# Two small reads of the first DFT pieces ahead of ScalarE's first instruction, in an FNet plus Mixer kernel

## Chip, cores and metric

The kernel runs on one core of one Trainium2 chip. The metric is device microseconds of one launch. The change is judged by the median of several runs of each kernel. 0.3% of the time before is 2.6 us.

## What is computed

One input x of 2048 tokens by 640 channels is normalized along its channels. The output is x plus a Fourier mixing of the normalized rows plus a token-mixing MLP of the same rows, all in 32-bit floats. Cut to what matters:

```python
xn = layernorm(x)                        # 2048 x 640
a  = xn @ dft_hid_re.T ; b = xn @ dft_hid_im.T
fnet = dft_seq_re @ a - dft_seq_im @ b   # dft_seq: 2048 x 2048 each
u  = gelu(xn.T @ w1 + b1)                # w1: 2048 x 1728
mlp = (u @ w2 + b2).T                    # w2: 1728 x 2048
out = x + fnet + mlp
```

## The kernel before

TensorE does nearly all the arithmetic. The kernel runs the Fourier mixing over the sequence first, then over the channels, then the two layers of the MLP ("up", "down"). Every weight piece is split into a rounded part ("hi", written by ScalarE, line 143) and a remainder ("lo", written by VectorE, line 146), and a product is three matmuls: hi by hi, hi by lo, lo by hi.

The DFT matrix of the sequence lies in device memory as `dft_seq[8][16][128][512]`. The first index is the column block of the real part (0 to 3) or the imaginary part (4 to 7), the second is a block of 128 rows. One piece is `dft_seq[c, i]`, 128 x 512 floats, 256 KB, contiguous; `dft_seq[0, 0]` and `dft_seq[1, 0]` are 4 MB apart. The change reads from these two. They are also the first two pieces that the kernel loads: `load(0)` (line 484) brings `dft_seq[0, 0]`, and the load of line 586 named `B11`, q = 0, brings `dft_seq[1, 0]`.

The order of the start is written out by hand in `START` (line 42), and the scheduler keeps it (`tc.manual_schedule()`). Each word is one step, and a step puts instructions on several engines. The words that matter here:

- `x0`: two transfers on SyncE's queue (SP), the left and right half of the first 128 rows of x (line 520). `b0`: the load of `dft_seq[0, 0]`. `W1-1-0`: the load of `dft_seq[1, 0]`. Then x1, b1, x2, W1-1-1, b2, W1-1-2, x3, b3 and so on, all on SP in this order.
- `M0 A0`: the moments of the first rows (VectorE, lines 218 and 221). `R0`: their inverse root (ScalarE, line 227). `G0 O0 V0`: small factors on GpSimd (lines 241, 238, 246, 247).
- `D0`: VectorE normalizes the first 256 columns of the first rows (line 383, `first_hi`). `H0`: ScalarE normalizes 128 more (line 275), with the offset that GpSimd computes in line 238.
- `T0`: hi of the first piece, half of it by ScalarE (line 143), half by VectorE (line 193). `B0`: its lo (VectorE, line 146). `T1`, `B1`: the same for the second piece, hi wholly by ScalarE.
- `P0-0-1`: the first six real matmuls (line 496), hi and lo of the piece against hi of the rows. `P1-0-1`: six for the second piece (line 656). `M1 A1`: the moments of the next rows. `L0`: lo of the first rows (VectorE, line 146, written to tile `n`). `P0-2`, `P1-2`: the passes that need L0.

Before these steps the kernel sets a few constants, lets ScalarE load its table with one tiny activation (line 135), and lets TensorE run 11 matmuls of a constant (line 140, `WARM`), which need no data and whose result is not used.

Of the kernel before, what the change touches and what calls it, by code (L numbers as in the profile page):

```python
# [8 lines left out]
F32 = mybir.dt.float32  # L9
# [5 lines left out]
P = 128  # L15
# [55 lines left out]
def fnet_plus_mixer(  # L71
# [30 lines left out]
    nc = tc.nc  # L102

    keep = ctx.enter_context(tc.tile_pool(name="keep", bufs=1))
# [25 lines left out]
    y_part = [[dram.tile([P, ND, CH], F32, name=f"y{m}{c}") for c in range(NC)] for m in range(2)]  # L130


    nc.vector.memset(one, 1.0)
    nc.gpsimd.memset(eps, EPS)
    nc.scalar.activation(one, one, AF.Abs_reciprocal_sqrt)
# [1165 lines left out]
```

## Time and profile before

| | us |
|---|---|
| median of 3 runs (lowest, highest) | 864.72 (864.64, 866.59) |
| the profiled execution's own time | 864.75 |
| its span, first to last instruction | 862.9 |
| outside the span | 1.85 |
| TensorE busy in the span | 858.4 |
| VectorE, ScalarE, GpSimd busy | 696.6, 529.1, 179.7 |

Times in the views are counted from the start of the span. PE is TensorE's matmul, PEld its weight load, DVE is VectorE, ACT ScalarE, POOL GpSimd. SPq and ACTq are the instruction queues of SyncE and ScalarE where they issue transfers. In a timeline, a row gives start, duration, engine, line, operation, tile written and tile read with their shapes, the number of instructions merged, and in brackets how long the engine had been idle before the row and what ended that idle time. The names in_x and in_dft_seq are the inputs in device memory, pieces the tile into which pieces of the DFT matrix are loaded, piece the tile with its hi and lo.

### The profile page before, as it was taken

The page shows a single profiled execution, that of the slowest core. Times are in us where ns is not written, and L with a number is a line of the kernel's source. Part 1 is how long each engine was busy: PE and PEld are TensorE (multiplying, and loading weights), DVE is VectorE, ACT ScalarE, POOL GpSimd, SP SyncE. Part 2 cuts the span into 40 slices and gives each one's busy share as a digit, 9 for nine tenths or more (in the row PEclk, how much of TensorE's full clock was granted, in tenths as well). Part 3 has the DMA queues.
Part 4 walks back from the last instruction along what each step waited for, and adds up shares of the span by engine and source line. Part 5 has one row for each costly group of instructions (what it writes and reads, how often), then busy time and mean ns, then how long its engine had stood idle before and what let it go on. Part 6 is the DMA issues. An engine that isn't in the chain of part 4 may idle for free.

```text
span 862.9 us, 13981 instructions
## 1 busy us (share of the span) xinstructions
PE 858.4 (99%) x4883; PEld 786.5 (91%) x4883; DVE 696.6 (81%) x1172; ACT 529.1 (61%) x987; POOL 179.7 (21%) x249
## 2 busy tenths in 40 slices
PE   9999999999999999999999999999999999999998
PEld 6888888888888888889999999999999999999998
DVE  7998868784757888877887788888678978897887
ACT  7766676755445555657565556676577856555654
POOL 5333222212121211122100101111312321101211
PEclk9999999999999999999999999999999999999999
DMA  8889594989593746779576766664688779766786
GB/s 316 287 223 322 126 298 130 246 196 297 139 262 61 200 97 144 171 128 211 122 170 169 159 147 181 196 180 152 148 178 186 169 213 243 184 139 130 157 167 149
DMA packets 93350, 159.44 MB, mean 185 GB/s; under 512 B 9408, under 2 KB 37824, under 8 KB 92928
## 3 DMA queue, kind: packets, MB, share of 16 engines
q0 software_dynamic: 26432, 60.40, 38.4%
q1 hardware_dynamic: 66704, 98.06, 35.3%
q8 instruction: 38, 0.62, 0.3%
q14 instruction: 32, 0.26, 0.1%
q10 hardware_dynamic: 144, 0.08, 0.0%
HBM read 102.05 MB, written 61.70 MB: 190 GB/s over the span
## 4 chain that ended last, share of the span: by engine, by line
PE 99%; DMA 0%; SPq 0%; ACT 0%; DVE 0%; issue 0%; DVEq 0%
PE psum L656 44%; PE psum L155 18%; PE psum L154 18%; PE psum L157 17%; PE psum L496 2%; DMA pieces<-in_dft_seq 0%; SPq L520 0%; ACT piece L143 0%; DVE pair L957 0%; DVEq L1297 0%
## 5 line engine op out<-in xcount | busy, mean ns | idle before, releaser
L146 DVE TENSOR_TENSOR piece<-pieces,piece 128x512 fp32r<-128x512 f32 (+4 forms) x514 | 338.7, 660 | 138.6 <-ACT piece L143 135.3
L143 ACT ACTIVATE piece<-pieces 128x512 fp32r<-128x512 f32 (+3 forms) x490 | 306.5, 626 | 230.8 <-PE psum L656 98.1
L656 PE MATMUL psum<-piece,n 128*128 128x512 f32 x1656 | 376.9, 389 | 0.0
L656 PEld LDWEIGHTS psum<-piece,n 128*128 128x128 f32 x1656 | 310.6, 188 | 65.1 <-DVE piece L146 0.4
L155 PE MATMUL psum<-sup,piece 128*128 128x320 f32 x392 | 120.8, 309 | 0.0
L154 PE MATMUL psum<-sup,piece 128*128 128x320 f32 x392 | 120.8, 309 | 0.0
L155 PE MATMUL psum<-sdown,piece 128*128 128x320 f32 x392 | 120.8, 309 | 0.0
L154 PE MATMUL psum<-sdown,piece 128*128 128x320 f32 x392 | 120.8, 309 | 0.0
L149 DVE TENSOR_TENSOR pieces<-pieces 128x512 f32<-128x512 f32 (+3 forms) x146 | 116.5, 803 | 2.8
L469 POOL DMA_DIRECT2D y<-c x76 | 65.5, 898 | 251.4 <-DVE c L692 132.4
L157 PE MATMUL psum<-sup,piece 128*128 128x320 f32 x368 | 113.7, 309 | 0.0
L157 PE MATMUL psum<-sdown,piece 128*128 128x320 f32 x368 | 113.7, 309 | 0.0
L157 PE MATMUL psum<-shid,piece 128*128 128x320 f32 x280 | 86.5, 309 | 0.0
L155 PE MATMUL psum<-shid,piece 128*128 128x320 f32 x280 | 86.5, 309 | 0.0
L154 PE MATMUL psum<-shid,piece 128*128 128x320 f32 x280 | 86.5, 309 | 0.0
L154 PEld LDWEIGHTS psum<-sup,piece 128*128 128x128 f32 x392 | 73.6, 188 | 0.0
L155 PEld LDWEIGHTS psum<-sdown,piece 128*128 128x128 f32 x392 | 73.6, 188 | 0.0
L155 PEld LDWEIGHTS psum<-sup,piece 128*128 128x128 f32 x392 | 73.6, 188 | 0.0
L154 PEld LDWEIGHTS psum<-sdown,piece 128*128 128x128 f32 x392 | 73.6, 188 | 0.0
L1038 POOL DMA_DIRECT2D out<-pair x38 | 33.0, 942 | 189.0 <-DVE pair L952 157.3
L965 ACT ACTIVATE pair<-psum 128x320 f32<-128x320 f32 x101 | 44.0, 436 | 42.4 <-PE psum L157 39.3
L157 PEld LDWEIGHTS psum<-sup,piece 128*128 128x128 f32 x368 | 69.1, 188 | 0.0
(120 smaller groups left out, 863.7 us busy)
## 6 DMA issues: line engine op xcount, KB each, us to landing
pieces<-in_dft_seq SPq DMA_DIRECT2D x136, 256.0 KB, 5.5
y<-c POOLq DMA_DIRECT2D x106, 256.0 KB, 6.1
pieces<-in_w SPq DMA_DIRECT2D x88, 256.0 KB, 4.0
out<-pair POOLq DMA_DIRECT2D x38, 320.0 KB, 5.3
pieces<-y SPq DMA_DIRECT2D x32, 320.0 KB, 4.2
pieces<-in_w SPq DMA_DIRECT2D x32, 192.0 KB, 3.0
up<-pair POOLq DMA_DIRECT2D x8, 640.0 KB, 3.4
pair<-in_x SPq DMA_DIRECT2D x12, 320.0 KB, 4.7
```

Source lines behind the costliest of these rows:

```text
L143: nc.scalar.activation(hi, src, AF.Copy)
L146: nc.vector.tensor_sub(lo, src, hi.bitcast(F32))
L149: nc.vector.tensor_sub(to, a, b)
L154: nc.tensor.matmul(psum, wh, mh, start=first, stop=False, skip_group_check=True)
L155: nc.tensor.matmul(psum, wh, ml, start=False, stop=last and wl is None, skip_group_check=True)
L157: nc.tensor.matmul(psum, wl, mh, start=False, stop=last, skip_group_check=True)
L469: nc.gpsimd.dma_start(y_part[m][c][:, j, :], t, accum_op=ALU.add)
L496: nc.tensor.matmul(to, (hi, hi, lo)[k], w[k % 2], start=k == 0 and i == 0, stop=k == 2 and i % 4 == 3, skip_group_check=True,)
L656: nc.tensor.matmul(to, (hi, hi, lo)[k], w[k % 2], start=k == 0 and begin, stop=k == 2 and q == 3, skip_group_check=True,)
L965: nc.scalar.activation(c, b, AF.Copy)
L1038: nc.gpsimd.dma_start(out_rows[ts[i]], c[:, i, :], accum_op=ALU.add)
```

## The change

Three lines are added ahead of the first instruction of the program's body. A small tile `touched` is taken in on-chip memory (16 partitions, two times 16 floats). ScalarE issues two transfers into it: 64 bytes out of every eighth row of `dft_seq[0, 0]`, 16 rows in all, and the same of `dft_seq[1, 0]`. No instruction reads the tile. They stand ahead of ScalarE's tiny activation and its table load. Nothing else is changed.

```diff
     y_part = [[dram.tile([P, ND, CH], F32, name=f"y{m}{c}") for c in range(NC)] for m in range(2)]
 
 
+    touched = keep.tile([P // 8, 2, 16], F32, name="touched")
+    for c in range(2):
+        nc.scalar.dma_start(touched[:, c, :], dft_seq[c, 0, ::8, :16])
     nc.vector.memset(one, 1.0)
     nc.gpsimd.memset(eps, EPS)
     nc.scalar.activation(one, one, AF.Abs_reciprocal_sqrt)
```

## Rows read from the trace of the kernel before

**Rows 1.** The page, chain that ended last, shares of the span by engine.
```profile
PE 99%; DMA 0%; SPq 0%; ACT 0%; DVE 0%; issue 0%; DVEq 0%
```

**Rows 2.** That chain in order of time: start us, us, what.
```profile
1.66 3.87 DMA pieces<-in_dft_seq
...
7.70 1.38 PE psum L656 x6
9.08 0.86 PE psum L496 x3
```

**Rows 3.** Busy time by stretch: length, then PE, PEld, DVE, ACT, POOL, PEclk, DMA share, GB/s.
```profile
10.60:859.50 848.90, 848.90 (x4855) 781.59 (x4853) 690.13 (x1156) 523.13 (x976) 175.48 (x234) 1.00 0.74 184
```

**Rows 4.** Timeline of PE, start of the span.
```profile
0.79 4.85 PE L140 MATMUL psum<-const-bfloat16-1.0 128*128 128x512 bf16 x11 [0.79 <-PEq L1290]
...
6.02 1.69 PE L496 MATMUL psum<-piece,n 128*128 128x512 f32 x6 [0.37 <-ACT piece L143]
```

**Rows 5.** Busy time by half microsecond, columns as in rows 3; read the last two.
```profile
2.00:2.50 0.50, 0.50 (x3) 0.20 (x2) 0.00 (x0) 0.24 (x2) 0.00 (x0) 1.00 0.71 259
...
3.00:3.50 0.50, 0.50 (x3) 0.17 (x2) 0.47 (x1) 0.00 (x0) 0.00 (x0) 1.00 1.14 159
3.50:4.00 0.50, 0.50 (x3) 0.15 (x1) 0.50 (x2) 0.00 (x0) 0.00 (x0) 1.00 0.88 270
4.00:4.50 0.50, 0.50 (x2) 0.15 (x1) 0.22 (x2) 0.15 (x1) 0.16 (x1) 1.00 1.02 197
4.50:5.00 0.50, 0.50 (x2) 0.15 (x1) 0.32 (x1) 0.15 (x1) 0.28 (x2) 1.00 0.99 346
...
10.00:20.00 10.00, 10.00 (x45) 8.21 (x44) 9.74 (x26) 8.57 (x18) 7.84 (x18) 1.00 1.05 393
```

**Rows 6.** Timeline of SP's queue, start of the span.
```profile
0.75 0.86 SPq L520 DMA_DIRECT2D x<-in_x  x2
...
3.55 0.43 SPq L522 DMA_DIRECT2D x<-in_x  x1
...
5.54 0.40 SPq L522 DMA_DIRECT2D x<-in_x  x1
6.17 0.42 SPq L484 DMA_DIRECT2D pieces<-in_dft_seq  x1
```

**Rows 7.** Timeline of ACT, start of the span.
```profile
0.75 1.28 ACT L135 ACT_TABLE_LOAD   x1 [0.75 <-PEq L1290]
2.05 0.20 ACT L135 ACTIVATE one<-one 128x1 f32<-128x1 f32 x1
4.35 0.29 ACT L227 ACTIVATE near<-mv,eps 128x1 f32<-128x1 f32 x1 [2.10 <-DVE mv L221]
...
5.87 0.48 ACT L275 ACTIVATE n<-x,near 128x128 fp32r<-128x128 f32 x1
6.25 0.62 ACT L143 ACTIVATE piece<-pieces 128x512 fp32r<-128x512 f32 x1
```

**Rows 8.** Timeline of DVE, start of the span.
```profile
3.04 0.97 DVE L218 BATCH_NORM_STATS2 st<-x 128x6 f32<-128x320 f32 x2 [2.15 <-DMA x<-in_x]
...
4.68 0.41 DVE L383 TENSOR_SCALAR n<-x,mv,near 128x256 fp32r<-128x256 f32 x1 [0.43 <-ACT near L227]
5.55 0.29 DVE L193 CAST piece<-pieces 128x256 fp32r<-128x256 f32 x1 [0.46 <-DMA pieces<-in_dft_seq]
...
7.51 0.88 DVE L218 BATCH_NORM_STATS2 st<-x 128x6 f32<-128x320 f32 x2
...
8.55 0.57 DVE L146 TENSOR_TENSOR n<-x,n 128x256 fp32r<-128x256 f32 x2
```

**Rows 9.** Timeline of POOL, start of the span.
```profile
4.75 0.39 POOL L238 TENSOR_SCALAR near<-mv,near 128x1 f32<-128x1 f32 x1 [0.22 <-ACT near L227]
```

**Rows 10.** Timeline of ACT's queue, end of the span.
```profile
860.23 0.37 ACTq L1128 DMA_DIRECT2D out<-pair  x1
```

**Rows 11.** Busy time by stretch at the end, columns as in rows 3; read PE and PEclk.
```profile
859.40:860.00 0.60, 0.21 (x2) 0.00 (x0) 0.35 (x2) 0.00 (x0) 0.00 (x0) 1.00 0.67 237
...
862.00:862.90 0.90, 0.00 (x0) 0.00 (x0) 0.00 (x0) 0.00 (x0) 0.00 (x0) 0.65 0.00 0
```

## The prediction

> **What bounds the kernel now.** I read the chain that ended last first, because it says which engine an edit must reach to matter. 99% of it is PE [rows 1]. The busy time by stretch then says from where on: from 10.60 to 859.50 us PE is busy for all of 848.90 us [rows 3]. Whatever the change does can therefore count only ahead of 10.6 us, by moving PE's real work earlier or later as a whole. At most what PE loses there can be won.
>
> PE runs its 11 matmuls of a constant from 0.79 to 5.64 us, stands idle for 0.37 us, and begins the real work at 6.02 us, when ScalarE has made the hi of the first piece [rows 4]. Six matmuls of 512 columns take 1.38 us in the next group [rows 2]. The first six took 1.69 us [rows 4], so 0.31 us is lost in them, waiting for the lo of the piece. The three of P0-2 take 0.86 us from 9.08 us [rows 2], where half of 1.38 is 0.69: 0.17 us lost, waiting for L0, whose two instructions start at 8.55 us on VectorE [rows 8]. Together PE loses 0.37 + 0.31 + 0.17 = 0.85 us after its constant matmuls. That is the ceiling of a gain that leaves the constant matmuls alone: 0.1% of the time.
>
> Behind the first wait is the load of `dft_seq[0, 0]`: issued at 1.66 us, landed 3.87 us later, at 5.53 us [rows 2]. The second piece is nearly as late. SP's issue of b3 at 6.17 us and that of x3 at 5.54 us [rows 6] come just when the transfers eight places before them have landed: x3 is SP's eleventh, b0 its third. So W1-1-0, the fourth, landed at about 6.16 us, and ScalarE takes it at 6.25 us [rows 7].
>
> The reason for the slow landing is seen in the DMA columns of the half microseconds [rows 5]. From 10 to 20 us the engines are busy (share 1.05) and move 393 GB/s. From 3.0 to 4.5 us they are as busy (1.14, 0.88, 1.02) but move 159, 270 and 197 GB/s. The missing parts, (1 - 159/393) x 0.5 + (1 - 270/393) x 0.5 + (1 - 197/393) x 0.5, are 0.30 + 0.16 + 0.25 = 0.71 us of the engines' time. In 4.5 to 5.0 us, at 346 GB/s, only 0.06 us is missing. The dip of 3.0 to 4.0 (0.46 us) falls where the first piece follows x0's 320 KB, that of 4.0 to 4.5 (0.25 us) where the second piece follows. I read the dips as a price of the first access to each of the two places, 4 MB apart. The rows fit this; they don't prove it.
>
> **The change, part by part.**
>
> ScalarE's two issues. ACT's own row for a transfer has 0.37 us [rows 10], SP's first two took 0.86 us together [rows 6]. So 0.74 to 0.86 us are put ahead of the table load, which took 1.28 us from 0.75 us, and the activation of 0.20 us behind it [rows 7]. They end at 3.0 to 3.1 us instead of 2.25. The next work of ScalarE starts at 4.35 us [rows 7]. The cover is ScalarE's idle time of 2.10 us ahead of it, of which some 1.3 us remain. The cost is nothing; without the cover it would be 0.86 us on the way to the inverse root.
>
> SP's places. If ACT's transfers share SP's turn of eight, x2 (SP's seventh) waits for the first read, W1-1-1 for the second. x2 is issued at 3.55 us [rows 6]. The reads are issued at about 0.75 and 1.2 us. By x0's first half, which was issued at 0.75 and there at 3.04 us (2.3 us) [rows 6, 8], they land at 3.1 and 3.5 us: no wait. By the first piece (3.87 us) they land at 4.6 and 5.1 us, and SP would stand for some 1.1 us with W1-1-1, b2 and all later loads behind it. The engines then still have the pieces and x1 in hand, as the second piece alone lands at 6.16 us, so this too costs next to nothing.
>
> What the reads do to the transfers. The first is issued 0.9 us ahead of the first piece (0.75 against 1.66 us). If the dips are first accesses, the pieces go at the full rate and land up to 0.71 us earlier. But the price does not vanish, it moves to 1.8 us, where x0 is on the same engines. Call d the time by which x0 comes later. Lower end: 0, if the stalls run beside x0's own start. Upper end: 0.71 us, if every stall stands in x0's way in full. The nearest row is x0's start itself, also a first access: 259 GB/s in 2.0 to 2.5 us [rows 5], a loss of (1 - 259/393) x 0.5 = 0.17 us. I take d = 0.2 us, since the reads start in the same microsecond as x0's and wait beside them.
>
> What is late next. With early pieces, VectorE's D0 ends at 4.68 + 0.41 = 5.09, its half of the hi at 5.09 + 0.29 = 5.38 us [rows 8]; later by d, that is 5.6 us, still inside the constant matmuls, so PE's 0.37 us go. But PE soon meets L0, at the end of the order H0 (ACT), T1 (ACT), B1, M1, A1, L0 (DVE). H0 starts at 5.87 us behind T0, T1 at 6.25 us [rows 7]. H0 needs the offset from GpSimd, ready at 4.75 + 0.39 = 5.14 us [rows 9], so it can move up by 0.73 - d. T1 needs the second piece, which comes up by 0.71 - d. M1 starts at 7.51 us right behind its neighbours [rows 8], and x1 moves up with the others. So L0, and PE with it, gains the smaller: 0.71 - d = 0.5 us. After that no wait on PE is known until the end [rows 3].
>
> The sum: 864.75 (the profiled execution: span 862.9 and 1.85 around it) - 0.5 = 864.2 us. Its own time is 0.03 us from the median, so the forecast for a median is the same, 864.2 us. The tile itself takes 128 bytes of a partition and has no reader; the last wait of the kernel comes 850 us after its transfers.
>
> **The rivals.**
>
> The stall is only moved, in full. If the reads hold up the engines as long as the pieces did, d = 0.71 us and the gain is 0. The second piece's stall (0.25 us) then also stands ahead of the first piece, which lay behind it before: b0 lands 0.25 us later. Time: 864.75 to 865.0 us. For it: the engines' share is near 1 while the rate is low [rows 5], so a stalled engine seems to do nothing else. Against it: x0's start costs only 0.17 us. The Trainium skill, "DMA: Bandwidth & Descriptors", section "Issuing engines are not separate DMA queues", speaks for this rival: transfers from ScalarE and SyncE end up on the same 16 engines and interleave, so issuing from a second one saves issue time alone. By that rule the time is this rival's, 864.75 to 865.0 us.
>
> The change doesn't do what it says. If the dips come from the load of the moment, or the reads warm nothing for the other queue, b0 and W1-1-0 are as slow as before and only d remains: 0 to 0.2 us, so 864.75 to 864.95 us. For it: nothing in the trace names the cause of the dips. Against it: from 10 to 20 us the same kind of loads run at 393 GB/s without a dip [rows 5]. The Trainium skill, "HBM Reference", section "Latency", gives 0.2 us for an access on average and 2 us under high load, which would make it load; the rows differ, as the slow stretch is the one that moves less.
>
> The clock falls, the one that ends clearly slower. The 11 constant matmuls take 4.85 us, 0.44 us each, the later ones of the same width 0.23 us [rows 4, 2]: the 1.2 and the 2.4 GHz level. At the end of the kernel PE is done at 859.6 us and the granted clock, a mean of 0.65 from 862.0 to 862.9, has fallen only then [rows 11], after at least 2.4 us of rest. If x0 or b0 came so late that PE rested for 2.4 us rather than 0.37, it would lose 2.0 us by the wait and, if the lower level lasted 4.85 us again, half of that: 864.75 + 2.0 + 2.4 = 869.2 us. It decides from 2.0 us of delay on, nearly three times the whole of the dips.
>
> **How the numbers follow.** Forecast (a gain of 0.25 to 0.85 us, d up to 0.45): 0.55. Stall moved in full: 0.20. No effect: 0.20. Clock: 0.02. What I haven't thought of: 0.03, of which 0.02 slower. The range reaches from the ceiling (864.75 - 0.85 = 863.9) to the full stall (865.0). The three runs before spread from 864.64 to 866.59, so a median of few runs may stray by some tenths: 863.6 to 865.4 us. About 0.3%, 2.6 us, is what a measurement of this kernel can tell from no change, so all but the last cases count as the same: faster 0.01, same 0.95, slower 0.04.
>
> **What would show it.** Right: the first piece lands by 4.9 us, the rate from 3.0 to 4.5 us is near 390 GB/s, a dip stands at 1.8 to 2.5 us instead, PE's idle time of 0.37 us is gone and L0 starts near 8.05 us. Full stall: x0's first statistics start 0.5 us or more after 3.04 us, and b0 lands no earlier. No effect: the same dips at 3.0 to 4.5 us. ScalarE's cover is wrong if the inverse root starts late while the moments were ready. The prediction is wrong altogether if PE waits after 10.6 us or its clock falls.

## The result, and the profile after

The change made the kernel slower: a median of 867.52 us (867.09 to 868.06, 9 runs) against 865.12 us (864.44 to 866.59, 9 runs) of the kernel before in the same rounds, a ratio of 1.0029 with an interval of 1.0020 to 1.0038. That is 2.4 us more, where 0.5 us less was forecast, and outside the range of 863.6 to 865.4 us. The profiled execution took 867.61 us with a span of 865.7 us, 2.8 us more than the span before.

The start looks as the forecast wanted it. All lines of the changed kernel behind the added ones count three higher; in the experiments it is as many as each adds. First PE's timeline, which answers to [rows 4], then ACT's [rows 7], then DVE's [rows 8], all of the changed kernel:

```profile
0.79 4.75 PE L143 MATMUL psum<-const-bfloat16-1.0 128*128 128x512 bf16 x11 [0.79 <-PEq L1293]
5.51 1.68 PE L499 MATMUL psum<-piece,n 128*128 128x512 f32 x6
```

```profile
0.75 0.89 ACTq L135 DMA_DIRECT2D touched<-in_dft_seq  x2
1.67 1.28 ACT L138 ACT_TABLE_LOAD   x1 [1.67 <-PEq L1293]
...
4.42 0.29 ACT L230 ACTIVATE near<-mv,eps 128x1 f32<-128x1 f32 x1 [1.26 <-DVE mv L224]
4.69 0.42 ACT L146 ACTIVATE piece<-pieces 128x256 fp32r<-128x256 f32 x1
5.25 0.49 ACT L278 ACTIVATE n<-x,near 128x128 fp32r<-128x128 f32 x1
5.65 0.62 ACT L146 ACTIVATE piece<-pieces 128x512 fp32r<-128x512 f32 x1
```

```profile
3.02 1.06 DVE L221 BATCH_NORM_STATS2 st<-x 128x6 f32<-128x320 f32 x2 [2.14 <-DMA x<-in_x]
...
8.11 0.63 DVE L149 TENSOR_TENSOR n<-x,n 128x256 fp32r<-128x256 f32 x2
```

The first piece is there when ScalarE asks for it at 4.69 us, PE begins its real work at 5.51 instead of 6.02 us, and L0 comes at 8.11 instead of 8.55 us. So some 3.2 us must have been lost later. No view of waits shows it. After the start of the program PE waits for nobody; this is the whole list of its waits in the changed kernel (what it waited for, us in total, times, longest):

```profile
PE psum L143 <- PEq L1293: 0.8, 1, 0.8
```

The loss is in the number of matmuls that a busy stretch holds. Busy time by stretch of the changed kernel, columns as in rows 3:

```profile
170.00:210.00 40.00, 40.00 (x178) 33.05 (x177) 26.86 (x42) 22.74 (x42) 10.53 (x13) 1.00 0.90 233
210.00:250.00 40.00, 40.00 (x176) 32.61 (x175) 28.47 (x38) 17.95 (x31) 5.96 (x7) 1.00 0.73 206
250.00:290.00 40.00, 40.00 (x175) 32.65 (x174) 28.14 (x37) 20.49 (x36) 5.17 (x6) 1.00 0.56 116
...
330.00:390.00 60.00, 60.00 (x262) 48.93 (x261) 48.16 (x74) 33.16 (x58) 12.88 (x15) 1.00 0.69 152
```

The same stretches of the kernel before:

```profile
170.00:210.00 40.00, 40.00 (x178) 33.10 (x178) 27.15 (x42) 23.13 (x42) 10.55 (x13) 1.00 0.93 232
210.00:250.00 40.00, 40.00 (x178) 33.14 (x177) 28.90 (x39) 18.30 (x31) 5.97 (x7) 1.00 0.73 204
250.00:290.00 40.00, 40.00 (x179) 33.10 (x178) 28.38 (x38) 20.52 (x37) 5.17 (x6) 1.00 0.56 119
...
330.00:390.00 60.00, 60.00 (x267) 49.64 (x266) 48.66 (x74) 33.67 (x59) 12.84 (x15) 1.00 0.73 161
```

Read the second number and the count behind it: PE is busy 100% of each stretch in both kernels, but from 210 us on 175 or 176 matmuls fit into 40 us instead of 178 or 179. The groups of the page say the same for the whole stage; the line of the changed kernel, then the one of before (busy us, mean ns of one):

```profile
L659 PE MATMUL psum<-piece,n 128*128 128x512 f32 x1656 | 380.1, 391 | 0.0
```

```profile
L656 PE MATMUL psum<-piece,n 128*128 128x512 f32 x1656 | 376.9, 389 | 0.0
```

3.2 us more for the same 1656 matmuls. These stretches lie in the second half of the sequence DFT, which in the changed kernel goes from 202 to 401 us. There the weights are parts of four tiles, n10 to n13. The views leave the numbers of tiles out, but the order in which the kernel issues its matmuls says which tile each of them took its weights from. Grouped by the tile that holds a matmul's weights, the mean time from one matmul's start to the next, from 27 to 389 us of the traces, is:

```
ns from start to start   n00    n01    n02    n03    n10    n11    n12    n13
before                   226.7  226.7  227.0  227.2  226.7  226.7  226.7  226.7
the change               226.7  226.7  226.7  227.3  233.0  232.7  228.5  227.7
matmuls                  189    190    198    198    210    210    204    201
```

210 x 6.3 + 210 x 6.0 + 204 x 1.8 + 201 x 1.0 ns are 3.2 us: the loss. n10 and n11 lie where x lay at the start (the slabs `slab4` and `slab5` of line 126), and these get their places in on-chip memory ahead of the added tile. Every other slab and the three tiles `piece`, which stream against the weights, get theirs behind it, in order. The tile holds 2 x 16 floats, 128 bytes of a partition. All sizes in between are multiples of 512 bytes, so before the change all weights and pieces began at the same offset within 512 bytes. Now n10 and n11 stand 128 bytes off the pieces, and the others stand as before. This is the theory that the experiments had to test against its rival, that the reads or the earlier start disturb the later stage.

### The profile page after: what moved, and what is told of

It reads as the page before. It is cut to its first block, busy times and chain, and to the rows that moved or that the text cites. A ratio compares the mean times of both kernels' runs of the same rounds, so it can differ in the third digit from the quotient of the medians.

```text
span 865.7 us, 13983 instructions
## 1 busy us (share of the span) xinstructions
PE 861.2 (99%) x4883; PEld 786.4 (91%) x4883; DVE 697.0 (81%) x1172; ACT 528.7 (61%) x987; POOL 179.8 (21%) x249
## 5 line engine op out<-in xcount | busy, mean ns | idle before, releaser
L158 PEld LDWEIGHTS psum<-sdown,piece 128*128 128x128 f32 x392 | 73.6, 188 | 0.0
L158 PEld LDWEIGHTS psum<-sup,piece 128*128 128x128 f32 x392 | 73.6, 188 | 0.0
L157 PEld LDWEIGHTS psum<-sdown,piece 128*128 128x128 f32 x392 | 73.6, 188 | 0.0
L157 PEld LDWEIGHTS psum<-sup,piece 128*128 128x128 f32 x392 | 73.6, 188 | 0.0
L160 PEld LDWEIGHTS psum<-sdown,piece 128*128 128x128 f32 x368 | 69.1, 188 | 0.4 <-DVE piece L149 0.4
```

The lines of the kernel that those rows point to most:

```text
L157: nc.tensor.matmul(psum, wh, mh, start=first, stop=False, skip_group_check=True)
L158: nc.tensor.matmul(psum, wh, ml, start=False, stop=last and wl is None, skip_group_check=True)
L160: nc.tensor.matmul(psum, wl, mh, start=False, stop=last, skip_group_check=True)
```

## The experiments

**The reads without the tile.**

```diff
+    for c in range(2):
+        nc.scalar.dma_start(again[: P // 8, c, :], dft_seq[c, 0, ::8, :16])
     nc.vector.memset(one, 1.0)
```

> The two reads as in the change, but into a tile that the kernel has anyway (again, written for the first time much later), so that no tile moves in on-chip memory. What the trace of the changed kernel shows: its real matmuls begin 0.5 us earlier, and the 3 us are lost between 217 and 390 us, where the matmuls that take their weights from two of the tiles (n10 and n11, the first rows' slabs of the second half) start every 233 ns instead of 227. Theory of the layout (the tile of 128 bytes moves all tiles that are allocated after it against those two slabs): no slow matmuls here, the earlier start stays, 0.4 to 0.6 us faster than before. Rival, the reads themselves or the earlier start disturb the later stage: 2 to 3 us slower than before, as the change.

Measured: 865.03 us (11 runs) against 864.76 us of before, a ratio of 1.0006 (0.9997 to 1.0015). The line of the page:

```profile
L658 PE MATMUL psum<-piece,n 128*128 128x512 f32 x1656 | 377.3, 390 | 0.0
```

All four tiles n10 to n13 are at 226.7 ns again. The slow stage is not the work of the reads. But the gain of 0.4 to 0.6 us isn't there either, and the profiled execution shows a start that went wrong. PE's timeline, then the busy time by stretch (read PE's count and PEclk, the granted clock):

```profile
0.79 3.82 PE L142 MATMUL psum<-const-bfloat16-1.0 128*128 128x512 bf16 x11 [0.79 <-PEq L1292]
6.57 2.72 PE L498 MATMUL psum<-piece,n 128*128 128x512 f32 x6 [1.95 <-ACT piece L145]
```

```profile
4.60:6.50 1.90, 0.01 (x1) 0.00 (x0) 0.73 (x2) 0.54 (x3) 1.25 (x5) 1.00 1.00 318
...
7.00:8.00 1.00, 1.00 (x4) 0.81 (x3) 0.78 (x2) 1.00 (x2) 0.00 (x0) 0.50 1.02 390
8.00:9.00 1.00, 1.00 (x4) 0.80 (x3) 0.97 (x4) 0.24 (x1) 0.00 (x0) 0.50 1.03 385
9.00:10.00 1.00, 1.00 (x4) 0.72 (x3) 0.68 (x3) 0.78 (x3) 0.63 (x3) 0.50 1.04 406
...
10.50:12.00 1.50, 1.50 (x8) 1.20 (x8) 1.26 (x4) 0.52 (x3) 0.76 (x3) 1.00 1.06 411
```

The first piece landed at 6.1 us here, later than before, PE rested 1.95 us, and from 7 to 10 us its granted clock is 0.50, the 1.2 GHz level. This one execution took 866.78 us.

**The tile without the reads.**

```diff
+    touched = keep.tile([P // 8, 2, 16], F32, name="touched")
+    nc.gpsimd.memset(touched, 0.0)
     nc.vector.memset(one, 1.0)
```

> The tile of the change at its place, without the reads; GpSimd sets it to zero with its first instruction so that it is used. Theory of the layout: the whole loss and none of the gain, 3 us slower than before, with matmuls at 233 ns where the weights come from n10 and n11. Rival, the reads or the earlier start: the time of before, within 0.5 us.

Measured: 867.78 us (5 runs) against 864.76, a ratio of 1.0034 (1.0021 to 1.0047): the whole loss, 3.0 us, without a read. Its line is the one of the change:

```profile
L658 PE MATMUL psum<-piece,n 128*128 128x512 f32 x1656 | 380.1, 391 | 0.0
```

By weights it shows 233.0, 232.7, 228.5 and 227.7 ns for n10 to n13, to the tenth the values of the change. The rival is out: the tile's place makes the matmuls slow, with no read at all.

**A tile of 512 bytes, and one of 256.** The edit is shown against the change; the reads still fill 16 floats of each half.

```diff
-    touched = keep.tile([P // 8, 2, 16], F32, name="touched")
+    touched = keep.tile([P // 8, 2, 64], F32, name="touched")
```

> The change with a larger tile: 512 bytes of a partition instead of 128, so that every tile behind it moves by 512 bytes. All of the weights, and the pieces that stream against them, then begin at the same offset within 512 bytes again, as before. Theory of the layout, in the form that the offset within 512 bytes counts: 0.4 to 0.6 us faster than before. Rival form, any move of the later tiles against the first two slabs costs: 2 to 3 us slower. Rival, the reads: 2 to 3 us slower.

Measured: 865.57 us (11 runs) against 864.76, a ratio of 1.0007 (0.9998 to 1.0016).

```profile
L659 PE MATMUL psum<-piece,n 128*128 128x512 f32 x1656 | 376.8, 389 | 0.0
```

The tile of 256 bytes has 32 floats where this one has 64.

> The change with a tile of 256 bytes of a partition. The matmuls alone showed 226.7 ns at 0, 256 and 512 bytes and 232 to 233 ns at 32, 64, 128 and 384. Theory of the layout with a period of 256 bytes: no slow matmuls, the time of the kernel with 512 bytes, between 0.5 us below and 0.8 us above before. Rival, a period of 512 bytes in the whole kernel: 3 us slower. For the reads: theory that they win the 0.5 us forecast: 864.2 to 864.5; rival, that they win nothing on average: at or up to 0.8 us above before.

Measured: 865.20 us (11 runs) against 864.63, a ratio of 1.0008 (0.9999 to 1.0017).

```profile
L659 PE MATMUL psum<-piece,n 128*128 128x512 f32 x1656 | 376.8, 389 | 0.0
```

A larger tile at the same place leaves the matmuls as fast as before. A move by 256 or 512 bytes is harmless, a move by 128 is not. The gain of 0.4 to 0.6 us that was expected with 512 bytes came with neither.

**The tile ahead of both slabs.** Again the edit is shown against the change.

```diff
+    touched = keep.tile([P // 8, 2, 16], F32, name="touched")
     x_slab = [
         keep.tile([P, 7, D], F32, name="x0", tag="slab4"), keep.tile([P, 1, D], F32, name="x1", tag="slab5"),
     ]
...
-    touched = keep.tile([P // 8, 2, 16], F32, name="touched")
```

> The change with the tile allocated ahead of the two slabs that hold x at the start (and n10, n11 later), so that all large tiles move by 128 bytes together and keep their distances. Theory of the layout, in the form that the distance between weights and streamed pieces counts: 0.4 to 0.6 us faster than before. Rival form, the absolute place of the pieces counts: 2 to 3 us slower. Rival, the reads: 2 to 3 us slower.

Measured: 865.50 us (11 runs) against 864.76, a ratio of 1.0008 (0.9999 to 1.0018).

```profile
L659 PE MATMUL psum<-piece,n 128*128 128x512 f32 x1656 | 376.8, 389 | 0.0
```

The pieces lie exactly where the change puts them, but the slabs have moved with them, and the line is within a tenth of the one of before. So it is the distance that counts, not the place. Here too the expected gain is missing.

**The tile between the slabs.** The same three lines, with the tile behind `x0` (slab4) and ahead of `x1` (slab5).

> The change with the tile allocated between the two slabs, so that n10 alone stands 128 bytes off the streamed pieces and n11 moves with them. Theory of the layout: the matmuls with weights from n10 alone start every 233 ns, half of the loss: 1.5 us slower than the kernel with the reads alone, 1.5 to 2.3 us slower than before. Rival form, the absolute place counts and not the distance: the whole loss of the change or none.

Measured: 867.35 us (10 runs) against 864.76, a ratio of 1.0026 (1.0017 to 1.0036), 2.6 us, more than the 1.5 to 2.3 us expected.

```profile
L658 PE MATMUL psum<-piece,n 128*128 128x512 f32 x1656 | 379.3, 391 | 0.0
```

n10 alone is out of place and shows 233.6 ns. But n11, which is in place, shows 230.4 ns: 210 x 6.9 + 210 x 3.7 ns are 2.2 of the 2.4 us that the line is above before. The time alone would not tell this from the rival's "whole loss of the change", which was 2.4 us; the split by tiles does, as n12 is back at 226.7 ns here. So the expectation of half the loss was wrong in size: matmuls that follow misplaced weights pay too, as n12 does behind n11 in the change.

**A pad ahead of the pieces.** The reads go into `again`, and the shift is put where it hits nearly everything.

```diff
     c_turn = [1]
+    pad = keep.tile([P, 32], F32, name="pad")
+    nc.gpsimd.memset(pad, 0.0)
```

> The reads go into the old tile, and 128 bytes that GpSimd sets to zero are allocated just ahead of the three tiles of the streamed pieces. So the weights of the whole first half (n00 to n03) and n10, n11 of the second stand 128 bytes off the pieces, n12 and n13 do not. Theory of the layout: some 800 matmuls of the first half and 400 of the second at 6 ns more, 7 us slower than before (5 to 9). Rival, something else in the second half is touched by the move: 2 to 3 us slower as the change.

Measured: 873.05 us (4 runs) against 864.76, a ratio of 1.0090 (1.0075 to 1.0105): 8.3 us for 128 bytes that nobody reads.

```profile
L660 PE MATMUL psum<-piece,n 128*128 128x512 f32 x1656 | 384.5, 394 | 0.0
```

By weights: 232.3 to 232.5 ns for n00 to n03, 233.0, 232.7, 228.5 and 227.7 for n10 to n13. 775 x 5.5 ns in the first half and the 3.2 us of the change are 7.5 us; the line has 7.6 us more than before. This is the dose that the theory demands.

**Matmuls alone.** A kernel of its own, in which eight groups of 60 matmuls run with no other engine at work.

```diff
+            def one(i, off):
+                at = off // 4 + (i % 4) * 128
+                return psum[i % 4], weights[:, at : at + P], moving[:, :512]
...
+            for i in range(N):
+                nc.tensor.matmul(*one(i, 128), start=True, stop=True)
```

> A kernel of matmuls alone, in which no other engine works at the same time: eight groups of 60 matmuls of 128 by 512 in the same 32-bit form, each with its own weight load, which stream the same tile. The groups differ in the byte offset at which the four weight blocks begin: 0, 32, 64, 128, 192, 256, 384 and 512 bytes past the place where the offset to the streamed tile is a multiple of 512 bytes. It computes nothing of the reference. Theory of the layout, in the form that the weight load and the stream of one and the same engine disturb each other: at 0 and 512 a matmul starts every 227 ns, at 128 every 232 ns or more; the other offsets show the period. Rival, the weights are disturbed by what ScalarE and VectorE write at the time: 227 ns in all eight groups.

PE's timeline; the lines 38 to 52 are the offsets 0, 32, 64, 128, 192, 256, 384 and 512, and the start of a group less that of the one before, by 60, is the time of one matmul:

```profile
20.42 13.77 PE L38 MATMUL ps<-moving,weights 128*128 128x512 f32 x60
34.03 14.15 PE L40 MATMUL ps<-moving,weights 128*128 128x512 f32 x60
48.02 14.16 PE L42 MATMUL ps<-moving,weights 128*128 128x512 f32 x60
62.02 14.11 PE L44 MATMUL ps<-moving,weights 128*128 128x512 f32 x60
75.97 13.90 PE L46 MATMUL ps<-moving,weights 128*128 128x512 f32 x60
89.70 13.77 PE L48 MATMUL ps<-moving,weights 128*128 128x512 f32 x60
103.31 14.11 PE L50 MATMUL ps<-moving,weights 128*128 128x512 f32 x60
117.26 13.77 PE L52 MATMUL ps<-moving,weights 128*128 128x512 f32 x60
```

At 0 bytes 13.61 us, 226.8 ns each, at 32, 64 and 128 bytes 233.2, 233.3 and 232.5 ns, at 192 bytes 228.8, at 256 bytes 226.8 and at 384 bytes 232.5 ns again; the group at 512 is as long as those at 0 and 256 (13.77 us). Among the offsets tried it repeats after 256 bytes, and PE does it to itself: neither VectorE's nor ScalarE's writes nor a transfer is needed. The rival of this run is out.

**Other widths, and mixed weights.** The same kernel with groups of 320, 384 and 256 columns at offsets 0 and 128 (lines 38 to 48), then 512 columns with the two offsets in turn (line 50) and in turn by sixes (line 52).

> Matmuls alone again, groups of 60 with their own weight loads, no other engine at work. Streams of 320, 384 and 256 columns, each with weights at 0 and at 128 bytes past a multiple of 512 bytes from the stream; then 512 columns with the weights at 0 and 128 in turn, one by one, and in turn by sixes. It computes nothing of the reference. Theory that the weight load hides behind a stream of 320 columns too and the two disturb each other: 320 columns at 147 ns with offset 0 and 150 ns or more with 128. Rival, which fits that the later stages of the changed kernel lost nothing (their streams have 320 columns): no difference at 320. In the mixed groups: if only a misplaced load costs, half of the 6 ns of the first micro kernel, 229.5 ns on average; more if the next one pays too, as n11 behind n10 in the kernel with the tile between.

```profile
19.24 8.96 PE L38 MATMUL ps<-moving,weights 128*128 128x320 f32 x60
28.04 8.96 PE L40 MATMUL ps<-moving,weights 128*128 128x320 f32 x60
36.84 10.57 PE L42 MATMUL ps<-moving,weights 128*128 128x384 f32 x60
47.24 10.72 PE L44 MATMUL ps<-moving,weights 128*128 128x384 f32 x60
57.80 7.35 PE L46 MATMUL ps<-moving,weights 128*128 128x256 f32 x60
64.99 7.28 PE L48 MATMUL ps<-moving,weights 128*128 128x256 f32 x60
72.11 14.09 PE L50 MATMUL ps<-moving,weights 128*128 128x512 f32 x60
86.04 14.02 PE L52 MATMUL ps<-moving,weights 128*128 128x512 f32 x60
```

320 columns take 146.7 ns at both offsets, 256 columns 119.8 and 118.7 ns, 384 columns 173.3 and 176.0 ns. So the streams of 384 and 512 columns pay and those of 320 don't. This fits the kernel's later stages, whose streams have 320 columns: from the end of the sequence DFT to the last matmul's start the change took 460.7 us, the kernel before 461.0. With the two offsets in turn every matmul pays (232.2 ns), not every second one: a misplaced load costs the neighbour too. By sixes the group is between (14.02 us, where a clean one takes 13.77 and a misplaced one 14.11).

The starts of single matmuls show a part of how the cost reaches a neighbour: a pace that has been disturbed comes back late. Behind misplaced weights, n12 in the change has at times one slow matmul (231 ns) and then 226 or 227 ns again, at times six slow ones in its run of six (236, 224, 231, 236, 228, 233 ns); n11 in the kernel with the tile between has nine of 224 to 236 ns in its run of nine. The same aftermath stands where no weights are misplaced. In the kernel before, one matmul of 251 ns at 35.25 us is followed by six of 228 to 236 ns, and in the first 30 matmuls of "Matmuls alone", all at offset 0, nine take 224 to 236 ns after the time of one has fallen from 427 ns. Why the pace comes back so late, and why the streams of 320 go free, these runs don't show.

**The first piece read twice.** The last question is about the start: whether a place that has been read is read faster again.

```diff
     with tc.manual_schedule():
+        nc.sync.dma_start(pieces[1][:, 1, 3, :], dft_seq[0, 0])
         for word in START.split():
```

> The kernel before with one more transfer as the first on SyncE's queue: the whole first piece, 256 KB, into a part of the pieces that is filled much later. Then x0 and the first piece again, as before. Theory that the slow stretch is the price of the first access to the place of the piece: it moves into the first transfer, and when the first piece comes again, from some 3.7 us on, the engines move it near 390 GB/s; only the second piece, 4 MB away, still costs. Rival, the dip does not belong to the place that is read: the rate falls below 200 GB/s for half a microsecond once more behind x0, as in all traces with the two small reads (148 to 175 GB/s from 3.0 to 3.5 us, 144 and 159 without them).

One run of 869.99 us; the transfer itself delays x0, so its time says nothing. The stretches of its start, columns as in rows 3; read the last two (DMA share, GB/s):

```profile
2.50:3.00 0.50, 0.50 (x3) 0.22 (x2) 0.00 (x0) 0.00 (x0) 0.00 (x0) 1.00 1.03 390
3.00:3.50 0.50, 0.50 (x3) 0.17 (x2) 0.00 (x0) 0.00 (x0) 0.00 (x0) 1.00 0.84 292
3.50:4.00 0.50, 0.50 (x4) 0.15 (x2) 0.14 (x1) 0.00 (x0) 0.00 (x0) 1.00 1.05 156
4.00:4.50 0.50, 0.50 (x4) 0.18 (x2) 0.35 (x1) 0.00 (x0) 0.00 (x0) 1.00 0.57 135
...
5.00:5.50 0.50, 0.00 (x0) 0.00 (x0) 0.00 (x0) 0.00 (x0) 0.00 (x0) 1.00 0.99 335
5.50:6.00 0.50, 0.00 (x0) 0.00 (x0) 0.46 (x1) 0.00 (x0) 0.00 (x0) 1.00 1.07 382
```

The dip, 156 and 135 GB/s from 3.5 to 4.5 us, now falls on x0, which comes second (its second half arrives at 5.54 us). From 5.5 us on, when the first piece comes again and behind it the second, of which nothing had been read, the rate is 382 GB/s. Neither theory is clean: a dip for whatever comes second fits, and so does a dip at a certain time after the start. It stays open.

## Why the prediction was wrong

**The step that failed is the sentence on the tile.** The prediction says: "The tile itself takes 128 bytes of a partition and has no reader". It looked for a reader of the tile and for a wait, found none, and put it at nothing in the sum. The tile's cost is that it moves what is allocated behind it: 3.2 us of slower matmuls, by the page's line, with or without the reads. It is shown from both sides: the tile alone gives the whole loss, the reads alone none of it, and the same tile at a place where the distances stay gives none.

**"Busy for all of 848.90 us" was read too far.** From [rows 3] the prediction concluded that behind 10.6 us nothing can change. That holds for waits. It doesn't hold for the rate: a matmul that takes 233 instead of 227 ns leaves PE just as busy. The sentence "The prediction is wrong altogether if PE waits after 10.6 us or its clock falls" left the third way out. The count behind the busy time, matmuls per stretch, is the witness.

**The second term that failed is the gain of the reads, 0.5 us: the chain was right, its cause was not.** In the profile of the change D0, H0, T1 and L0 moved up much as worked out: L0 at 8.11 us where near 8.05 was forecast, PE's idle time of 0.37 us gone. But that was one execution, and a lucky one. In seven profiles with the reads (the change and six experiments), ScalarE starts on the first piece at 4.69, 6.10, 5.52, 5.43, 5.00, 6.17 and 5.49 us, 5.49 us on average; in the two without them but with the same order of transfers (before and the tile alone) at 5.55 and 5.60 us: the change's 4.69 us is the earliest of all nine. And the dip that the reads should have removed [rows 5] is there each time. The change's own half microseconds:

```profile
3.00:3.50 0.50, 0.50 (x3) 0.18 (x2) 0.48 (x1) 0.17 (x1) 0.00 (x0) 1.00 1.06 175
3.50:4.00 0.50, 0.50 (x3) 0.15 (x1) 0.43 (x2) 0.00 (x0) 0.00 (x0) 1.00 0.93 332
4.00:4.50 0.50, 0.50 (x2) 0.15 (x1) 0.29 (x2) 0.08 (x1) 0.09 (x1) 1.00 1.06 262
```

175 GB/s from 3.0 to 3.5 us, 148 to 181 in all seven, against 159 and 144 without the reads. From 3.5 to 4.5 us the tile alone, without a read, had 340 and 254 GB/s, so the better rates there are no merit of the reads. The rival "The change doesn't do what it says" was the right one for this half, and 0.20 was too little for it: the reading of the dips as first accesses was a guess, and the text said so, but 0.71 us hung on it. Measured, the term is no gain: the four kernels with reads and with the distances kept came out 0.3 to 0.8 us above before, each with an interval that reaches just below 1; a small cost of the reads is likely, but not shown.

**d was small.** x0's first half came at 3.02 us (3.04 before), the inverse root at 4.42 (4.35 before): 0.07 us, where 0.2 was taken. The rival of a stall moved in full is out in these traces.

**ScalarE and SP were right.** Two issues took 0.89 us (0.74 to 0.86 forecast), the table load began at 1.67 us, and 1.26 us of idle time were left ahead of the inverse root (1.3 forecast). SP issued x2 and W1-1-1 at 3.56 and 4.03 us, as before.

**The clock rival is not what made the change slower, but it does happen.** In the change the granted clock is 1.00 in all the stretches above. In the one execution of the reads alone PE rested 1.95 us, where the rival reckoned with 2.4 us, and the granted clock was 0.50 from 7 to 10 us. In the run that reads the first piece twice PE rested 2.67 us, and the granted clock was 0.50 from 7.5 to 10.5 us. At the tenth real matmul the execution of the reads alone was 2.1 us behind before, of which 0.55 us are the later start (6.57 against 6.02 us).

**The range** had room for what was named, and 0.02 for something unnamed that is slower. An edit that moves the addresses of most tiles deserved more than that. By the prediction's own measure, 2.6 us, the 2.4 us measured still count as the same; that they are a loss is told by the interval of the ratio, 1.0020 to 1.0038, and by the count of matmuls.

## What to carry to other kernels

A new tile is an edit to every tile that is allocated behind it: before an on-chip tile is added to a tuned kernel, see which tiles it moves against which, and use a tile that is there already, or pad the new one to a harmless size (here 256 bytes). A pair that matters is a matmul's weights and its streamed operand; in this kernel a distance off a multiple of 256 bytes cost up to 3% of each matmul of 512 columns. When a kernel gets slower and no wait has grown, count the instructions in equal stretches and group them by what they read. And a gain read from one profile at the start of a kernel isn't one until several executions show it.

## What the runs showed of the hardware

- The time from one matmul to the next, each with its own weight load, depends on how far its weights lie from its streamed operand in on-chip memory: 226.8 ns for 512 columns at distances of 0 and 256 bytes, 228.8 at 192, 232.5 to 233.3 at 32, 64, 128 and 384, with all other engines at rest. The Trainium skill, "SBUF — State Buffer", section "Who interferes with whom", gives TensorE two read ports that are independent, one for the streamed operand and one for the weights. The measurement differs, and here it decides: moving the weights alone by 128 bytes costs 5.7 ns a matmul, so the two reads are not independent. The section also says that TensorE never waits on anyone; for other engines no run here tests that.
- It depends on the width: nothing at 320 columns (146.7 ns at both offsets), 2.7 ns at 384 (173.3 and 176.0), 5.7 ns at 512 (226.8 and 232.5).
- After a disturbance the pace of the matmuls comes back late even with well-placed weights: six matmuls of 228 to 236 ns behind one of 251 ns in the kernel before, nine of 224 to 236 ns at the start of the matmuls alone, against 226 to 227 ns undisturbed.
- The time that the 11 constant matmuls take differs between executions of the same start: 3.82, 4.01, 4.12, 4.25, 4.50, 4.75 and 4.85 us were seen. In the execution with the shortest of them the first piece was late too, PE rested 1.95 us, and from 7 to 10 us its granted clock was 0.50.
